# VectorE's two masked pieces ahead of ScalarE's four negated copies in each group of key products

## The chip, the cores and the metric

The kernel runs on one core of a Trainium2 chip. The metric is the device time of one execution in microseconds (us); times given for a kernel are medians over runs. TensorE multiplies matrices into PSUM, VectorE and ScalarE read PSUM and work element by element, GpSimd (POOL) works on SBUF alone, and SyncE (SP) issues transfers. In the rows PE is TensorE, PEld its weight loads, DVE VectorE and ACT ScalarE. Each engine works through its own list of instructions in order, and waits on semaphores for the others.

## The reference

A recurrent attention over 768 steps, whose state is a 40x40 matrix for each of 4 batches and 8 heads, and two gated layers behind it:

```python
for t in range(S):
    y[:, :, t] = np.einsum('bhd,bhde->bhe', rt, state)
    Sa = np.einsum('bhde,bhe->bhd', state, at)
    state_decay = state * wt[:, :, None, :] - np.einsum('bhd,bhe->bhde', Sa, bt)
    state = state_decay + np.einsum('bhd,bhe->bhde', vt, kt)
...
x = (silu(x @ w_gate) * (x @ w_val)) @ w_out        # 3072 x 320, d_ff 1536
x = (sigmoid(x @ w_gate) * (x @ w_val)) @ w_out
```

## The kernel before, in words

The 768 steps are cut into 12 chunks of 64. For a chunk, `prep_a` scales the keys by products of the decays, transposes them and forms **key products** (L486): four groups of four 128x128 products, each group in one PSUM tile `kps`. All chunks but the first use one PSUM bank (`mm`) for them, so the next group's products wait until the group before has been read out. Two things are read out of each group. ScalarE writes negated copies of blocks on the diagonal into `bn` (L495: 32 partitions by 4x64, L496: 32 by 4x32, for each of the two heads). VectorE writes masked pieces into `lq` (L498: 64 partitions by 4x64, one for each head).

`prep_b` inverts 1 + `bn` by blocks on VectorE: `halves` for chunks 0 to 2 (begins with the transpose L554, works in L567 and L573, ends with `x1t` at L578), `whole` for chunks 3 to 11 (begins with the transpose L512, works in 15 pairs of L526 and L532, ends with `x1t` at L536). TensorE makes `zps` and `xps` (L647) from it, and ScalarE writes the inverse X (L662). `chain` is the recurrence from chunk to chunk: products `qps` (L692, from the fourth chunk on L766), copies `qs` on ScalarE (L779), products `ups` with X (L710, later L787), copies of those (L800, L803), products `sps`, and the new state. `post` computes the chunk's outputs (aps L861, yps L892, `ysb` L906). Between them TensorE works off the first gated layer for the chunk before (`gv` L1112, `po` L1128), and VectorE, ScalarE and POOL turn float64 weights into pairs of fp32r tiles (on VectorE L1014, L1015, L1019, L1020, four passes for a third of a weight tile). When the 12 chunks are done the rest of the first layer and the second layer run as one stream of products (L1167, L1128).

Python generators are merged by fixed weights (`merge`), which gives each instruction a priority. A scheduler then lays the instructions out on the engines with those priorities and its own cost model, and places the semaphores. It lets two engines that read the same PSUM bank do so only one after the other, in the order in which they are written in the code. So the order of lines sets a chain of waits within a group, and moves what the scheduler puts around it.

Of the kernel before, what the change touches and what calls it, by code (L numbers as in the profile page):

```python
# [42 lines left out]
def attention(ctx, tc, st, ident, ins, banks, extra, early, more):  # L43
# [4 lines left out]
    nc = tc.nc  # L48
# [40 lines left out]
    QUAD = [slice(32 * j, 32 * j + 32) for j in range(4)]  # L89
# [128 lines left out]
    inv, done, out = {}, set(), {}  # L218
# [61 lines left out]
    for hs in HALF:  # L280
        nc.gpsimd.affine_select(
            out=mask[hs, :],
            in_=mask[hs, :],
# [20 lines left out]
    for u in range(2):  # L304
        nc.vector.tensor_reduce(
            out=odd[:, u : u + 1], in_=ident.rearrange("p (c u) -> p u c", u=2)[:, u], axis=AX.X, op=ALU.add
# [7 lines left out]
    for l in range(2):  # L314
        for z in range(2):
            nc.vector.tensor_reduce(
                out=sel[:, 2 * l + z : 2 * l + z + 1],
                in_=ident.rearrange("p (h l z c) -> p l z h c", h=2, l=2, z=2)[:, l, z],
# [131 lines left out]
    def prep_a(m):  # L450
        if 0 < m < FS:
            yield from scanned(m)
            if m == FS - 1:
                done.add("scans")
        elif m:
            while m not in rd:
                yield
            en = ends(m)
            s = scaled(m)
            next(s)  # L460
            next(en)
            yield
            yield from s
        tk = tkb[m % 3]
        while m > 2 and ("q", m - 3) not in done:
            yield
        for bp in range(2):
            ps = tr4(lambda n: an[:, 4 * bp + n])
            for h2 in range(2):
                e = E40[h2]  # L470
                nc.scalar.copy(
                    out=lq[m % 3][e, 8 * bp : 8 * bp + 8, h2], in_=ps[e].rearrange("p n (c t) -> p (n c) t", c=2)
                )
            yield
        if m >= FS:
            pends[m] = next(en)
        bn = wk.tile([P, NS, C], F32, tag="bn", name="bn", bufs=2)
        for g4 in range(4):
            q = slice(4 * g4, 4 * g4 + 4)
            ps = tr4(lambda n: tk[:, 4 * g4 + n], ("joined", None, "merged", None)[g4] if m == 1 else None)  # L480
            kbt = wk.tile([P, 4, P], F32, tag="kbt", name="kbt", bufs=1)
            nc.scalar.copy(out=kbt[0:PW], in_=ps[0:PW])
            pool, tag = ((pmm, "mm"), (pzy, "zy"), (pqu, "qu"), (po, "po1"))[g4 if m == 0 else 0]
            kps = pool.tile([P, 4, 2, C], F32, tag=tag, name="kps")
            for n in range(4):
                nc.tensor.matmul(  # L486
                    kps[:, n].rearrange("p h t -> p (h t)"),
                    lhsT=kbt[0:PW, n, :],
                    rhs=lq[m % 3][0:PW, 4 * g4 + n].rearrange("p h t -> p (h t)"),
                    start=True,  # L490
                    stop=True,
                )
            for h2 in range(2):
                lo, hi = QUAD[2 * h2], QUAD[2 * h2 + 1]
                nc.scalar.mul(out=bn[lo, q, :], in_=kps[lo, :, h2, :], mul=-1.0)  # L495
                nc.scalar.mul(out=bn[hi, q, 0:32], in_=kps[hi, :, h2, 32:64], mul=-1.0)  # L496
                o = HALF[1 - h2]
                nc.vector.tensor_tensor(  # L498
                    out=lq[m % 3][o, q, h2, :],
                    in0=kps[o, :, h2, :],  # L500
                    in1=mask[o, None, :].to_broadcast([64, 4, C]),
                    op=ALU.mult,
                )
            yield
        inv[m] = bn

# [447 lines left out]
    if NCH > 1:  # L954
        start.append((prep_a(1), *QA))
# [601 lines left out]
```

## Time and profile before

| | |
|---|---|
| time, median of 3 runs | 1272.05 us (1271.22 to 1274.35) |
| the profiled execution's own time | 1274.74 us |
| its span, first to last instruction | 1272.7 us |
| TensorE busy, matmul rows | 1185.2 us (93%) |
| VectorE busy | 687.8 us (54%) |
| ScalarE busy | 592.3 us (47%) |
| mean granted TensorE clock | 0.956 of full speed |

The profile is of one execution. Its rows are read in us from the span's start. In rows of waits "A <- B" means that A's engine stood idle until B had ended. A TensorE that is busy throughout a stretch bounds it; where it has idle time, the wait that ended last in front of it does.

### The profile page before, as it was taken

The page shows a single profiled execution, that of the slowest core. Times are in us where ns is not written, and L with a number is a line of the kernel's source. Part 1 is how long each engine was busy: PE and PEld are TensorE (multiplying, and loading weights), DVE is VectorE, ACT ScalarE, POOL GpSimd, SP SyncE. Part 2 cuts the span into 40 slices and gives each one's busy share as a digit, 9 for nine tenths or more (in the row PEclk, how much of TensorE's full clock was granted, in tenths as well). Part 3 has the DMA queues.
Part 4 walks back from the last instruction along what each step waited for, and adds up shares of the span by engine and source line. Part 5 has one row for each costly group of instructions (what it writes and reads, how often), then busy time and mean ns, then how long its engine had stood idle before and what let it go on. Part 6 is the DMA issues. An engine that isn't in the chain of part 4 may idle for free.

```text
span 1272.7 us, 31392 instructions
## 1 busy us (share of the span) xinstructions
PE 1185.2 (93%) x12545; PEld 1070.1 (84%) x12545; DVE 687.8 (54%) x1432; ACT 592.3 (47%) x1447; POOL 557.7 (44%) x749
## 2 busy tenths in 40 slices
PE   5598799999999999899999999999999999999997
PEld 4487588889889988788898888888888888888886
DVE  6867769876678667956867544467121212121111
ACT  8465546556655575455433433445232323232222
POOL 5744842233223224356855766676232223222221
PEclk8678868999999999999999999999999999999998
DMA  7444664544655555343464543323010101000001
GB/s 221 131 131 148 146 168 123 123 99 111 153 121 115 115 136 122 88 106 110 125 237 126 182 160 127 107 88 91 2 46 1 46 1 35 1 21 1 22 1 25
DMA packets 180460, 124.38 MB, mean 98 GB/s; under 512 B 134608, under 2 KB 160208, under 8 KB 179536
## 3 DMA queue, kind: packets, MB, share of 16 engines
q1 hardware_dynamic: 180144, 122.11, 35.5%
q8 instruction: 101, 1.65, 0.5%
q14 instruction: 55, 0.45, 0.1%
q10 hardware_dynamic: 160, 0.16, 0.1%
HBM read 90.81 MB, written 31.43 MB: 96 GB/s over the span
## 4 chain that ended last, share of the span: by engine, by line
PE 60%; DVE 22%; ACT 8%; issue 4%; DMA 2%; POOL 2%; SPq 0%; DVEq 0%; ACTq 0%; POOLq 0%
PE g L1167 31%; PE po L1128 16%; DVE pr L526 4%; PE gv L1112 4%; DVE part L532 3%; PE kps L486 2%; PE aps L861 2%; PE tp L371 2%; DVE lq L498 1%; PE ups L787 1%; ACT bn L496 1%; DVE am L870 1%; DVE dt L1015 1%; ACT bn L495 1%; ACT part L751 1%
## 5 line engine op out<-in xcount | busy, mean ns | idle before, releaser
L1167 PE MATMUL g<-x,w 128*128 128x512 f32 (+1 forms) x1792 | 419.8, 385 | 2.1 <-DVE g L1174 2.0
L1167 PEld LDWEIGHTS g<-x,w 128*128 128x128 f32 x1792 | 323.3, 188 | 62.8 <-issue 2.8
L1176 POOL TENSOR_TENSOR hl<-g,hh 128x256 fp32r<-128x256 f32 x216 | 162.1, 756 | 281.8 <-ACT hh L1175 253.9
L1174 DVE TENSOR_TENSOR g<-g,g 128x256 f32<-128x256 f32 x216 | 82.1, 419 | 342.4 <-PE g L1167 340.1
L1128 PE MATMUL po<-w,hh 128*128 128x320 f32 x1152 | 233.6, 311 | 0.9 <-ACT hh L1118 0.8
L1128 PEld LDWEIGHTS po<-w,hh 128*128 128x128 f32 x1152 | 187.0, 188 | 9.9 <-ACT hh L1118 1.0
L1175 ACT CAST hh<-g 128x256 fp32r<-128x256 f32 x216 | 86.9, 406 | 179.4 <-PE po L1128 169.7
L1112 PE MATMUL gv<-x,w 128*128 128x256 f32 x1152 | 165.6, 291 | 3.8 <-DVE g L1117 2.5
L1128 PE MATMUL po<-w,hl 128*128 128x320 f32 x576 | 151.1, 313 | 3.6 <-POOL hl L1119 3.5
L1112 PEld LDWEIGHTS gv<-x,w 128*128 128x128 f32 x1152 | 147.7, 192 | 6.8 <-DVE g L1117 3.9
L1171 ACT ACTIVATE g<-g 128x256 f32<-128x256 f32 x216 | 73.0, 382 | 149.5 <-PE g L1167 143.1
L1119 POOL TENSOR_TENSOR hl<-g,hh 128x256 fp32r<-128x256 f32 x72 | 62.8, 872 | 128.8 <-ACT hh L1118 127.9
L1032 POOL TENSOR_TENSOR dt<-dt,w 128x384 f32<-128x384 f32 (+1 forms) x72 | 80.3, 1116 | 87.5 <-ACT w L1030 42.7
L1128 PEld LDWEIGHTS po<-w,hl 128*128 128x128 f32 x576 | 99.6, 188 | 5.6 <-POOL hl L1119 5.2
L498 DVE TENSOR_TENSOR lq<-kps,part 64x256 f32<-64x256 f32 x96 | 40.5, 422 | 85.9 <-ACT bn L496 67.0
L526 DVE TENSOR_TENSOR pr<-part,sn 128x4 f32<-128x4 f32 (+4 forms) x135 | 76.2, 565 | 3.7
L1014 DVE TENSOR_SCALAR dt<-dt 128x384 int32<-128x384 int32 (+1 forms) x72 | 41.8, 580 | 52.8 <-POOL dt L1011 52.5
L486 PE MATMUL kps<-lq,kbt 104*128 104x128 f32 x384 | 61.3, 309 | 8.9 <-DVE lq L498 6.4
L532 DVE TENSOR_REDUCE part<-pr 128x2 f32<-128x4 f32 (+4 forms) x135 | 66.6, 493 | 2.8
L486 PEld LDWEIGHTS kps<-lq,kbt 104*128 104x128 f32 x384 | 53.4, 215 | 13.2 <-PE yps L892 4.1
L861 PE MATMUL aps<-rbd,ut 104*128 104x128 f32 x384 | 57.1, 295 | 6.1 <-DVE ysb L906 3.6
L1030 ACT CAST w<-dt 128x384 fp32r<-128x384 f32 (+1 forms) x72 | 35.6, 495 | 55.3 <-DVE dt L1015 48.2
(185 smaller groups left out, 1711.4 us busy)
## 6 DMA issues: line engine op xcount, KB each, us to landing
raw<-in_w_dram SPq DMA_DIRECT2D x48, 384.0 KB
xd<-x SPq DMA_DIRECT2D x12, 896.0 KB
x<-xd SPq DMA_DIRECT2D x11, 896.0 KB
raw<-in_w_dram SPq DMA_DIRECT2D x24, 320.0 KB
ld<-in_a_kb_dram SPq DMA_DIRECT2D x22, 320.0 KB
ld<-rd SPq DMA_DIRECT2D x64, 80.0 KB
pn<-pd SPq DMA_DIRECT2D x32, 160.0 KB
ld<-in_a_a_dram SPq DMA_DIRECT2D x12, 320.0 KB
```

What stands on the lines that cost most here:

```text
L486: nc.tensor.matmul(kps[:, n].rearrange("p h t -> p (h t)"), lhsT=kbt[0:PW, n, :], rhs=lq[m % 3][0:PW, 4 * g4 + n].rearrange("p h t -> p (h ...
L526: nc.vector.tensor_tensor(out=o, in0=xs[:, 0:kk, None, 0:n].to_broadcast([P, kk, 2, n]), in1=sn[:, None, n : n + 2, 0:n].to_broadcast([P, ...
L532: nc.vector.tensor_reduce(out=xs[:, 0:kk, n : n + 2], in_=o, axis=AX.X, op=ALU.add)
L861: nc.tensor.matmul(aps[:, n, h2], lhsT=ut[0:PW, x, 2 * h2 : 2 * h2 + 2].rearrange("p u s -> p (u s)"), rhs=rbd[0:PW, x, h2].rearrange("p b ...
L1032: sub(out=tf, in0=tf, in1=w.bitcast(F32), op=ALU.subtract)
L1112: nc.tensor.matmul(gv[n], lhsT=p, rhs=q, start=e == 0, stop=e == len(seq) - 1)
L1128: self.nc.tensor.matmul(ops[u], lhsT=p[:, us], rhs=q, start=first and n == 0, stop=last and n == 2)
L1167: nc.tensor.matmul(gv[k][:, 0:n], lhsT=p, rhs=cols(at), start=e == 0, stop=e == len(seq) - 1)
L1171: nc.scalar.activation(out=g[j], in_=gv[0][:, j], func=AF.Silu if silu else AF.Sigmoid)
L1174: nc.vector.tensor_tensor(out=g[j], in0=gv[1][:, j], in1=g[j], op=ALU.mult)
L1175: nc.scalar.copy(out=hh, in_=g[j])
L1176: self.heng.tensor_tensor(out=hl, in0=g[j], in1=hh.bitcast(F32), op=ALU.subtract)
```

## The change

In each group the loop over the two heads is split into two loops: first both masked pieces on VectorE, then the four negated copies on ScalarE. What each instruction reads and writes is the same.

```diff
             for h2 in range(2):
-                lo, hi = QUAD[2 * h2], QUAD[2 * h2 + 1]
-                nc.scalar.mul(out=bn[lo, q, :], in_=kps[lo, :, h2, :], mul=-1.0)
-                nc.scalar.mul(out=bn[hi, q, 0:32], in_=kps[hi, :, h2, 32:64], mul=-1.0)
                 o = HALF[1 - h2]
                 nc.vector.tensor_tensor(
                     out=lq[m % 3][o, q, h2, :],
...
                     op=ALU.mult,
                 )
+            for h2 in range(2):
+                lo, hi = QUAD[2 * h2], QUAD[2 * h2 + 1]
+                nc.scalar.mul(out=bn[lo, q, :], in_=kps[lo, :, h2, :], mul=-1.0)
+                nc.scalar.mul(out=bn[hi, q, 0:32], in_=kps[hi, :, h2, 32:64], mul=-1.0)
             yield
```

In the changed file the masked piece stands at L495, the copies at L503 and L504, and every later line is one higher. The instructions and their number are the same on every engine; their order differs from the first chunk until the last chunks.

VectorE in the opening of the program, before: the eight masked pieces of chunk 0 (`lq_192`), passes of the weight conversion (`dt`, `ds`) and scaled keys of chunk 1 (`part_88`, `tkb_90`), up to the transpose with which the inversion of chunk 0 begins (L554).

```order
L155 TENSOR_SCALAR s_1209<-s_1209 128x10x64
L498 TENSOR_TENSOR lq_192<-kps,part_86 64x4x64 x5
L418 TENSOR_TENSOR part_88<-ld,dtp 128x8x2x32
L498 TENSOR_TENSOR lq_192<-kps,part_86 64x4x64
L1014 TENSOR_SCALAR dt<-dt 128x384
L1015 SCALAR_TENSOR_TENSOR dt<-raw,dt 128x384
L498 TENSOR_TENSOR lq_192<-kps,part_86 64x4x64
L425 TENSOR_TENSOR tkb_90<-ld,dtp 128x8x2x16 x2
L1019 TENSOR_SCALAR ds<-dt 128x384
L498 TENSOR_TENSOR lq_192<-kps,part_86 64x4x64
L554 STREAM_TRANSPOSE sn<-bn 128x512
```

The same place of the changed kernel (the transpose is L555 there):

```order
L495 TENSOR_TENSOR lq_192<-kps,part_86 64x4x64 x2
L155 TENSOR_SCALAR s_1209<-s_1209 128x10x64
L495 TENSOR_TENSOR lq_192<-kps,part_86 64x4x64 x4
L418 TENSOR_TENSOR part_88<-ld,dtp 128x8x2x32
L495 TENSOR_TENSOR lq_192<-kps,part_86 64x4x64 x2
L425 TENSOR_TENSOR tkb_90<-ld,dtp 128x8x2x16 x2
L1015 TENSOR_SCALAR dt<-dt 128x384
L555 STREAM_TRANSPOSE sn<-bn 128x512
```

The masked pieces go in pairs, and two weight passes have moved behind the transpose.

VectorE at the end of an inversion in the middle of the program, before: the last steps of the inversion (L526, L532), between them the masked pieces of two groups of the chunk after (`lq_192`), outputs (`ysb`) and the last step's transpose.

```order
L532 TENSOR_REDUCE part_88<-pr 128x13x2
L498 TENSOR_TENSOR lq_192<-kps,part_86 64x4x64
L526 TENSOR_TENSOR pr<-part_88,sn 128x28x28
L498 TENSOR_TENSOR lq_192<-kps,part_86 64x4x64
L532 TENSOR_REDUCE part_88<-pr 128x14x2
L906 TENSOR_TENSOR ysb<-yps,pn 128x320
L906 TENSOR_TENSOR ysb<-yps,pn 128x64
L526 TENSOR_TENSOR pr<-part_88,sn 128x900
L498 TENSOR_TENSOR lq_192<-kps,part_86 64x4x64
L532 TENSOR_REDUCE part_88<-pr 128x15x2
```

The same inversion of the changed kernel (L527 and L533 are its steps, L907 the outputs):

```order
L533 TENSOR_REDUCE part_88<-pr 128x13x2
L871 TENSOR_TENSOR am<-aps,part_86 128x512
L527 TENSOR_TENSOR pr<-part_88,sn 128x28x28
L495 TENSOR_TENSOR lq_192<-kps,part_86 64x4x64 x2
L533 TENSOR_REDUCE part_88<-pr 128x14x2
L527 TENSOR_TENSOR pr<-part_88,sn 128x900
L907 TENSOR_TENSOR ysb<-yps,pn 128x320
L907 TENSOR_TENSOR ysb<-yps,pn 128x64
L533 TENSOR_REDUCE part_88<-pr 128x15x2
L495 TENSOR_TENSOR lq_192<-kps,part_86 64x4x64 x2
```

The first pair stands where the second piece stood, and the second pair behind the last step.

ScalarE at the same time, before, up to the copies `qs` from which the recurrence goes on (L779); `x` are casts for the gated layer.

```order
L495 ACTIVATE bn<-kps 32x256
L496 ACTIVATE bn<-kps 32x4x32
L1064 CAST x<-xtp 128x512
L1068 CAST x<-xtp 64x256
L1069 CAST x<-xtp 64x256
L495 ACTIVATE bn<-kps 32x256
L496 ACTIVATE bn<-kps 32x4x32
L779 COPY qs<-qps 128x320 x2
```

The same place of the changed kernel (`qs` is L780 there):

```order
L1065 CAST x<-xtp 128x512
L1069 CAST x<-xtp 64x256
L1070 CAST x<-xtp 64x256
L503 ACTIVATE bn<-kps 32x256
L504 ACTIVATE bn<-kps 32x4x32
L503 ACTIVATE bn<-kps 32x256
L504 ACTIVATE bn<-kps 32x4x32
L780 COPY qs<-qps 128x320 x2
```

All four copies of the second group now stand straight ahead of `qs`, and they come behind that group's pair on VectorE.

## Rows read from the trace of the kernel before

**Rows 1.** The page, chain that ended last, shares of the span by engine.

```profile
PE 60%; DVE 22%; ACT 8%; issue 4%; DMA 2%; POOL 2%; SPq 0%; DVEq 0%; ACTq 0%; POOLq 0%
```

**Rows 2.** Windows: stretch, length, busy us by engine, granted clock, DMA share, GB/s.

```profile
32.00:64.00 32.00, 16.11 (x478) 14.26 (x478) 27.47 (x57) 13.51 (x32) 24.11 (x31) 0.66 0.46 130
900.00:1000.00 100.00, 100.00 (x521) 87.59 (x520) 17.76 (x44) 31.61 (x86) 29.02 (x44) 1.00 0.06 15
```

**Rows 3.** Windows from the start, and of one period, ups to ups.

```profile
0.00:244.40 244.40, 193.79 (x3297) 172.89 (x3299) 185.91 (x380) 145.34 (x321) 126.99 (x173) 0.79 0.55 147
...
371.24:412.88 41.64, 40.20 (x671) 37.73 (x673) 31.01 (x64) 25.30 (x63) 12.29 (x15) 1.00 0.55 128
```

**Rows 4.** Waits of the whole span: us in total, times, longest.

```profile
DVE lq L498 <- ACT bn L496: 67.0, 45, 5.1
...
ACT bn L495 <- PE kps L486: 36.0, 26, 2.4
...
PE hps L588 <- DVE x1t L578: 9.1, 1, 9.1
...
PE kps L486 <- DVE lq L498: 6.4, 12, 1.1
```

**Rows 5.** VectorE's waits from 22 to 42 us.

```profile
DVE lq L498 <- ACT bn L496: 3.5, 4, 1.7
```

**Rows 6.** Instructions of tile kps: durations min/median/max in ns.

```profile
L495 ACT ACTIVATE bn<-kps x96: 357/375/379, 25.3 to 512.8; 32x256 f32<-32x256 f32 x96
L496 ACT ACTIVATE bn<-kps x96: 268/270/272, 25.6 to 513.1; 32x128 f32<-32x128 f32 x96
L498 DVE TENSOR_TENSOR lq<-kps,part x96: 406/420/429, 27.2 to 513.4; 64x256 f32<-64x256 f32 x96
```

**Rows 7.** Timeline of TensorE in one period: start, us, instructions, idle before.

```profile
373.18 1.16 PE L486 MATMUL kps<-lq,kbt 104*128 104x128 f32 x8
...
378.18 0.65 PE L371 MATMUL tp<-ident,tkb 128*104 128x128 f32 x4 [0.51 <-ACT part L755]
...
407.18 1.13 PE L486 MATMUL kps<-lq,kbt 104*128 104x128 f32 x8 [0.43 <-DVE lq L498]
...
412.81 0.89 PE L787 MATMUL ups<-qs,part 64*64 64x40 f32 x23
```

**Rows 8.** Timeline of ScalarE in the same period.

```profile
376.75 0.38 ACT L495 ACTIVATE bn<-kps 32x256 f32<-32x256 f32 x1 [0.49 <-DVE lq L498]
...
399.28 1.19 ACT L662 ACTIVATE part<-xps 32x512 f32<-32x512 f32 x2
...
411.09 0.75 ACT L779 COPY qs<-qps 128x320 f32<-128x320 f32 x2
```

**Rows 9.** Timeline of VectorE in the same period.

```profile
376.28 0.43 DVE L498 TENSOR_TENSOR lq<-kps,part 64x256 f32<-64x256 f32 x1 [4.65 <-ACT bn L496]
...
405.58 0.98 DVE L526 TENSOR_TENSOR pr<-part,sn 128x784 f32<-128x784 f32 x1
406.62 0.42 DVE L498 TENSOR_TENSOR lq<-kps,part 64x256 f32<-64x256 f32 x1
...
409.93 1.09 DVE L532 TENSOR_REDUCE part<-pr 128x30 f32<-128x900 f32 x1
```

**Rows 10.** Timeline of VectorE and TensorE in the opening.

```profile
35.42 0.56 DVE L1015 SCALAR_TENSOR_TENSOR dt<-raw,dt 128x384 int32<-128x384 int32 x1
...
37.14 0.35 DVE L1019 TENSOR_SCALAR ds<-dt 128x384 int32<-128x384 int32 x1
...
37.74 1.05 DVE L554 STREAM_TRANSPOSE sn<-bn 128x512 f32<-128x512 f32 x1
...
68.84 0.43 DVE L498 TENSOR_TENSOR lq<-kps,part 64x256 f32<-64x256 f32 x1
...
72.53 3.23 PE L710 MATMUL ups<-qs,part 64*64 64x40 f32 x56
...
87.80 1.06 DVE L554 STREAM_TRANSPOSE sn<-bn 128x512 f32<-128x512 f32 x1
```

## The prediction

> **What bounds the kernel now.** I read the chain that ended last first: TensorE holds 60% of it, VectorE 22%, ScalarE 8% [rows 1]. Then the windows, since that is a mean over stages. In the late stretch TensorE is busy for 100.00 of 100.00 us at full clock [rows 2]; nothing there waits, and the change touches nothing there. In the middle, one chunk of the recurrence after the other takes 41.64 us, of which TensorE works 40.20 [rows 3]; the period shown is one of six alike between 244.4 and 496.2 us. So 1.44 us a period are to be had there, at most some 9 in all. The first 244.40 us are another matter: TensorE works 193.79 of them [rows 3] and stands for 50.6, and between 32 and 64 us it is busy for half of the time at a clock of 0.66, while VectorE is busy for 27.47 of 32 [rows 2]. There VectorE's order decides.
>
> Last the waits. VectorE stood idle 67.0 us in front of masked pieces until a copy L496 had ended, and ScalarE 36.0 us in front of copies until products had ended [rows 4]. The first is not a loss of 67.0: most of it is time in which the group's products, too, were not there yet. What reaches TensorE is smaller: 6.4 us in 12 waits of products for a masked piece that frees the bank, and 9.1 us for the `x1t` of chunk 0 [rows 4].
>
> **What the change does, and what it costs.** No work is added: 96 pieces of 0.42 us, 96 copies of 0.375 and 96 of 0.27 [rows 6] before and after. A group is read out in 2 x 0.42 + 2 x 0.645 = 2.13 us either way, since the two engines take turns at the bank. The turns fall from three to one. A turn itself costs little: the piece that starts at 376.28 takes 0.43 [rows 9], and the copy behind it starts at 376.75 [rows 8], 0.04 us after its end; two turns fewer are some 0.08 us a group. What counts is what each engine does while it waits for its turn, and where the scheduler puts the group. Three places:
>
> Opening, chunk 0. The transposes of its inversion start at 37.74 [rows 10]. Two weight passes (0.56 and 0.35 us, rows at 35.42 and 37.14) go from in front of it to behind it: 0.9 us sooner [rows 10]. Of the 3.5 us that VectorE stood in front of masked pieces here [rows 5] the alternation goes, but the products of the third and fourth group still have to come; I take 0.8 of it (bounds 0 and 3.5). So the inversion starts some 1.7 us sooner, and `x1t`, for which TensorE waits 9.1 us [rows 4], about 2 sooner, as two of the passes that stood in front of it now follow.
>
> It is then given back. The products `ups` of chunk 0 start at 72.53 [rows 10], and need X. In the changed order the copies of X stand behind the second group's four negated copies, these behind the pair, and the pair behind four weight passes, which end at 68.8 today, where the first piece starts at 68.84 [rows 10]. 68.84 + 0.84 for the pair + 1.29 for the copies + 1.2 for X (the 1.19 of the later form [rows 8]) is 72.2. So `ups` start as now. Next, though, the fourth group of chunk 1 and its pair stand ahead of the sums of the state on VectorE, not behind them, and the inversion of chunk 1 that starts at 87.80 [rows 10] can start up to 4 us sooner. Outputs behind it move the other way in VectorE's order, and the products that need their bank with them. I carry half, 2.0 us; the bounds are 0 and 6 (4, and half as much again when chunk 2 repeats it).
>
> Middle, second group of a period. Its products wait for the bank until 407.18, 0.43 us idle [rows 7], because the second piece of the first group runs from 406.62 to 407.04 behind a step of the inversion that ended at 406.56 [rows 9]. In the changed kernel the pair stands behind that same step. Without the first piece in front of it the step ends some 0.45 sooner, at 406.1; then 0.84 for the pair and 1.29 for the four copies with their gaps: 408.3. The products start 1.2 us later than now. Should the inversion begin sooner, which it can by 0.35 as its last wait ahead is shorter, it is 0.9 later. Against that: at 376.75 ScalarE stands 0.49 us in front of a copy for its turn [rows 8], and 0.51 us of TensorE's idle time at 378.18 follow from it, through a copy that ScalarE makes right behind [rows 7]. The third group's products start at 373.18 [rows 7] and are there by 374.4, when VectorE is idle (4.65 us of idle time in front of the piece at 376.28 [rows 9]); the pair is done before ScalarE comes to the copies, so that the 0.5 goes. Net +0.4 to +0.7 us a period; I take 0.5. Three periods of the changed order have this form; one has the pair a step earlier (the bank is free at 407.3, not later than now), and gains 0.4; three have their products in another order, which I price at nothing (bounds -0.5 and +0.9, the best and the worst of the other forms). Together +1.1 us.
>
> Late stretch: 0, for TensorE's full windows cover it [rows 2].
>
> Sum: -2.0 + 1.1 = -0.9 us. On the profiled execution's 1274.74 us that is 1273.8; that execution lies 2.7 above the median of the runs, 1272.05. The forecast is made for the median: 1271.1 us. A difference below 0.3%, 3.8 us, can't be told from none.
>
> **The rivals.** *The opening carries on (faster).* The sooner start of chunk 1's inversion passes to chunk 2 and to the first regular period, because VectorE and ScalarE and not TensorE's work set the end there: 50.6 us of standing in [rows 3] speak for it. Against it: POOL's weight work and transfers have their own pace in the opening. Opening -6, middle 0: 1266 us.
>
> *The pair holds up the recurrence (slower).* In the changed order all four copies of the second group stand ahead of `qs`, and the pair they wait for stands behind the last step of the inversion, which runs from 409.93 to 411.02 [rows 9]. Pair 0.84, copies 1.29: 413.2, then 0.75 for `qs`, which now starts at 411.09 [rows 8]; less 0.35 for an inversion that begins sooner, and less 0.4 for the piece no longer on the way, it is 413.2. `ups` start at 412.81 now [rows 7]. So `qs` and the second group's wait both come out 0.4 to 0.9 later, and since the inversion's start hangs on the fourth group, which follows `ups`, the delay adds up by period. Seven periods at 0.9 are 6.3 us; with nothing gained in the opening, 1278.3 us. It decides from 0.55 us a period (3.8 by 7). Speaking against it: the 0.5 us that each period gets back between `ups` and the fourth group. The Trainium skill says the same of the mechanism (PSUM — Partial Sum Buffer, Engine vs sequencer instructions): ScalarE's and VectorE's queues are strict first-in first-out, so whatever stands behind a waiting copy waits too. The trace agrees: the copies behind the one at 376.75 ran late by its 0.49 us [rows 8].
>
> *It moves nothing that counts.* The scheduler has shifted hundreds of rows, but TensorE's work is the same and nearly fills the middle. This is my forecast's own case.
>
> **How the numbers follow.** Within 0.3% (1268.3 to 1275.8): 0.47; the carried gain and what lies beyond 0.3%: 0.28; the held-up recurrence: 0.25. The range reaches down to 1264.5, a little past the carried gain, and up to 1278, nearly the seven long periods; it leaves out the two cases together (0.2). The likeliest case's own range is 1268.3 to 1275.8.
>
> **What would show it.** Right: VectorE's wait for L496 is gone from the list of waits, and ScalarE waits for masked pieces instead; the first transposes start near 36.0 and the second near 84; the `ups` of the first chunk start at 72 to 73; the period is 41.3 to 42.2 us, with about 1 us of idle TensorE in front of the second group and none at the third group's transposes; the first regular `ups` start about 242 in place of 244.4. Wrong: a period over 42.2 us makes it slower, a start of the regular part before 239 makes it faster; a late stretch that is not the same length would mean that I looked in the wrong place.

## The result and the profile after

The changed kernel takes 1288.61 us (median of 4 runs, 1286.98 to 1292.85) against 1272.64 of the kernel before: a ratio of 1.0126, interval 1.011 to 1.0142. The forecast was 1271.1 in a range of 1264.5 to 1278. The profiled execution spans 1286.8 us, 14.1 more than before. In the changed kernel the masked pieces stand at L495, the copies at L503 and L504, and everything behind them has moved down by one line.

First the windows that answer to [rows 2, 3]: stretch, length, busy us by engine, granted clock, DMA share, GB/s.

```profile
0.00:254.60 254.60, 192.03 (x3308) 171.16 (x3308) 189.23 (x381) 145.20 (x322) 125.04 (x173) 0.81 0.52 142
32.00:64.00 32.00, 15.65 (x418) 13.86 (x414) 27.48 (x55) 12.64 (x31) 23.53 (x30) 0.66 0.46 124
254.60:295.80 41.20, 39.43 (x656) 37.22 (x656) 30.03 (x61) 22.99 (x56) 11.79 (x14) 0.96 0.56 128
295.80:341.00 45.20, 42.41 (x688) 39.55 (x687) 32.20 (x66) 27.31 (x69) 12.09 (x14) 1.00 0.54 123
341.00:385.70 44.70, 41.04 (x657) 38.79 (x656) 30.94 (x63) 24.63 (x62) 11.23 (x14) 0.92 0.54 115
385.70:428.00 42.30, 40.50 (x672) 37.81 (x671) 31.70 (x63) 24.90 (x63) 12.97 (x15) 1.00 0.46 109
...
470.22:513.44 43.22, 41.61 (x671) 39.20 (x670) 31.71 (x63) 25.35 (x64) 12.28 (x15) 0.96 0.50 114
513.44:562.29 48.85, 43.09 (x650) 39.91 (x650) 37.50 (x75) 23.24 (x57) 19.14 (x26) 0.86 0.37 101
900.00:1000.00 100.00, 100.00 (x523) 87.71 (x523) 19.85 (x48) 30.84 (x84) 31.23 (x45) 1.00 0.06 15
```

The first regular `ups` start at 254.60 in place of 244.3, 10.3 us late. The last ones start at 604.0 in place of 585.5, so that another 8.2 is lost between. From there to the end it is 682.8 us against 687.2 before: 4.4 come back. The late stretch is full, as it was. Period by period, from the first regular `ups` to the last (us):

| period | 1 | 2 | 3 | 4 | 5 | 6 | 7 | 8 |
|---|---|---|---|---|---|---|---|---|
| before | 43.55 | 41.66 | 41.63 | 41.64 | 41.65 | 41.64 | 46.37 | 43.00 |
| changed | 41.12 | 45.22 | 44.75 | 42.25 | 42.25 | 43.22 | 48.85 | 41.75 |

So plain periods are 42.25 long in place of 41.6. In the changed kernel the first has some 16 products of TensorE fewer in it, and the second as many more; the first, third and sixth have a granted clock below 1.00, and the seventh 0.86. The seventh of the kernel before, to be read against the 513.44 line above:

```profile
496.10:542.47 46.37, 39.65 (x650) 37.05 (x650) 37.08 (x76) 23.27 (x57) 18.71 (x26) 0.96 0.40 111
```

The waits that answer to [rows 4] (us in total, times, longest):

```profile
DVE lq L495 <- PE kps L486: 49.3, 24, 5.1
...
ACT bn L503 <- DVE lq L495: 19.1, 22, 2.1
...
PE kps L486 <- ACT bn L504: 13.4, 13, 3.6
...
PE hps L589 <- DVE x1t L579: 8.6, 1, 8.6
...
PE yps L893 <- DVE am L871: 3.3, 5, 0.8
```

VectorE's wait for a negated copy, 67.0 us before, is gone from the list, and its products are what VectorE waits for now. Where TensorE lost 6.4 us to masked pieces it now loses 13.4 to the copies behind them. And there is a wait that the forecast did not have: `yps` for `am`, the mask of `post`, 3.3 us in 5 times (1.0 in 2 before).

One plain period shows both. VectorE of the changed kernel (start, us, instructions, idle before), to be read against [rows 9]:

```profile
416.92 0.86 DVE L527 TENSOR_TENSOR pr<-part,sn 128x676 f32<-128x676 f32 x1
417.81 0.86 DVE L533 TENSOR_REDUCE part<-pr 128x26 f32<-128x676 f32 x1
418.59 0.68 DVE L871 TENSOR_TENSOR am<-aps,part 128x512 f32<-128x512 f32 x1
419.19 0.97 DVE L527 TENSOR_TENSOR pr<-part,sn 128x784 f32<-128x784 f32 x1
420.18 0.86 DVE L495 TENSOR_TENSOR lq<-kps,part 64x256 f32<-64x256 f32 x2
```

TensorE in the same stretch, against [rows 7]:

```profile
419.32 1.13 PE L893 MATMUL yps<-part,rbd 104*64 104x40 f32 x32 [0.77 <-DVE am L871]
...
422.45 1.16 PE L486 MATMUL kps<-lq,kbt 104*128 104x128 f32 x8 [0.81 <-ACT bn L504]
```

The second mask of `post` stands behind the reduction of 26 columns (in the kernel before it stands ahead of it), and TensorE waits 0.77 us for it. The pair stands behind the next step, the product of 784 columns; before the change only the second piece stood behind it [rows 9]. TensorE waits 0.81 us for the four copies that follow the pair, where it waited 0.43 [rows 7]. Of nine inversions with this step, the mask stands behind the reduction in none of the kernel before and in six of the changed one.

The opening, to be read against [rows 10]. VectorE, the two inversions' transposes:

```profile
36.29 1.08 DVE L555 STREAM_TRANSPOSE sn<-bn 128x512 f32<-128x512 f32 x1
...
89.44 1.06 DVE L555 STREAM_TRANSPOSE sn<-bn 128x512 f32<-128x512 f32 x1 [1.46 <-ACT bn L504]
```

TensorE, the first recurrence products of chunk 0:

```profile
73.50 1.80 PE L711 MATMUL ups<-qs,part 64*64 64x40 f32 x22 [0.29 <-ACT part L663]
```

The first inversion starts 1.45 us sooner, near the 1.7 of the forecast; in e17 below, with the same opening order, it starts at 37.87, so that a difference of this size is not clear of what executions differ by. `ups` start 1.0 later all the same, and the second inversion 1.6 later, where up to 4 sooner was forecast. The delay grows from there: the third inversion starts 4.2 later (130.51 for 126.34), the fourth 7.5 (178.91 for 171.45), and the first regular `ups` 10.3.

### The profile page after: what moved, and what is told of

Read it like the earlier page. It is cut to its first block, busy times and chain, and to the rows that moved or that the text cites. A ratio compares the mean times of both kernels' runs of the same rounds, so it can differ in the third digit from the quotient of the medians.

```text
span 1286.8 us, 31385 instructions
## 1 busy us (share of the span) xinstructions
PE 1190.5 (93%) x12545; PEld 1075.2 (84%) x12545; DVE 693.3 (54%) x1432; ACT 590.3 (46%) x1447; POOL 555.8 (43%) x749
## 4 chain that ended last, share of the span: by engine, by line
PE 63%; DVE 20%; ACT 7%; DMA 4%; issue 4%; POOL 2%; SPq 0%; ACTq 0%; DVEq 0%; POOLq 0%
PE g L1168 30%; PE po L1129 16%; PE gv L1113 5%; DVE pr L527 4%; DVE part L533 3%; PE kps L486 2%; PE aps L862 2%; PE tp L371 1%; PE qps L767 1%; PE ups L788 1%; DMA wt<-in_a_w_dram 1%; DVE am L871 1%; PE yps L893 1%; ACT bn L503 1%; DVE part L826 1%
## 5 line engine op out<-in xcount | busy, mean ns | idle before, releaser
L1177 POOL TENSOR_TENSOR hl<-g,hh 128x256 fp32r<-128x256 f32 x216 | 162.6, 758 | 282.4 <-ACT hh L1176 254.1
L527 DVE TENSOR_TENSOR pr<-part,sn 128x4 f32<-128x4 f32 (+4 forms) x135 | 78.0, 578 | 3.8
L486 PE MATMUL kps<-lq,kbt 104*128 104x128 f32 x384 | 62.5, 313 | 16.8 <-ACT bn L504 13.4
L533 DVE TENSOR_REDUCE part<-pr 128x2 f32<-128x4 f32 (+4 forms) x135 | 66.4, 492 | 2.7
L495 DVE TENSOR_TENSOR lq<-kps,part 64x256 f32<-64x256 f32 x96 | 40.5, 422 | 50.8 <-PE kps L486 49.3
L1009 ACT ACTIVATE dt<-raw 128x384 f32<-128x384 f32 (+1 forms) x72 | 38.3, 534 | 51.8 <-POOL w L1037 30.2
```

Of the source, the lines that this page charges most:

```text
L486: nc.tensor.matmul(kps[:, n].rearrange("p h t -> p (h t)"), lhsT=kbt[0:PW, n, :], rhs=lq[m % 3][0:PW, 4 * g4 + n].rearrange("p h t -> p (h ...
L527: nc.vector.tensor_tensor(out=o, in0=xs[:, 0:kk, None, 0:n].to_broadcast([P, kk, 2, n]), in1=sn[:, None, n : n + 2, 0:n].to_broadcast([P, ...
L533: nc.vector.tensor_reduce(out=xs[:, 0:kk, n : n + 2], in_=o, axis=AX.X, op=ALU.add)
L1177: self.heng.tensor_tensor(out=hl, in0=g[j], in1=hh.bitcast(F32), op=ALU.subtract)
```

## The experiments

Seventeen kernels, all compared with the kernel before on the same chip. In most, a group's copies and piece of head `h2` are made two small functions, and one line chooses their order by chunk `m` or group `g4` (here for e1):

```diff
-            for h2 in range(2):
+            for step, h2 in (((piece, 0), (piece, 1), (copies, 0), (copies, 1)) if m < 5 else ((copies, 0), (piece, 0), (copies, 1), (piece, 1))):
+                step(h2)
```

What came out; the ratio is to the kernel before in the same set of runs, "first" and "last" are the starts of the first and the last regular `ups` in us, "plain" is the length of the plain periods in the profile, the short ones that are nearly alike, in brackets those of others between the first period and the last two. The last three columns are of one profiled execution, which for e7 is 5.7 us and for e9 4.5 us slower than the median beside it, for the others at most 2.5 off it.

| run | pieces first where, or edit | median us | ratio, interval | first | plain | last |
|---|---|---|---|---|---|---|
| before | | 1272.64 | 1 | 244.3 | 41.6 | 585.5 |
| changed | always | 1288.61 | 1.0126, 1.0110 to 1.0142 | 254.6 | 42.3 (45.2, 44.7, 43.2) | 604.0 |
| e1_early | `m < 5` | 1277.84 | 1.0046, 1.0032 to 1.0061 | 254.4 | 41.7 | 591.8 |
| e2_late | `m >= 5` | 1282.97 | 1.0079, 1.0048 to 1.0110 | 244.4 | 42.2 (44.6) | 597.1 |
| e3_chunks01 | `m in (0, 1)` | 1291.83 | 1.0152, 1.0119 to 1.0185 | 253.6 | 41.6 | 600.6 |
| e4_chunks12 | `m in (1, 2)` | 1275.52 | 1.0024, 1.0005 to 1.0043 | 247.5 | 41.6 | 588.6 |
| e5_first_group | `m >= 5 and g4 == 0` | 1276.18 | 1.0028, 1.0013 to 1.0043 | 244.1 | 41.5 | 585.7 |
| e6_second_group | `m >= 5 and g4 == 1` | 1279.16 | 1.0057, 1.0033 to 1.0081 | 239.4 | 41.3 (42.4, 45.3) | 585.0 |
| e7_copies_pair | `m >= 5`, copies first | 1282.57 | 1.0073, 1.0048 to 1.0099 | 243.4 | 42.0 (45.0, 42.6) | 597.1 |
| e8_not_first_group | `m >= 5 and g4` | 1282.93 | 1.0078, 1.0055 to 1.0102 | 242.7 | 41.4 (43.4, 44.5) | 591.7 |
| e9_mask_ahead | `m >= 5`, mask placed | 1279.80 | 1.0062, 1.0040 to 1.0084 | 245.2 | 41.1 (42.6, 44.9) | 590.8 |
| e10_pass_behind | always, one pass placed | 1302.26 | 1.0236, 1.0209 to 1.0263 | 257.7 | 42.2 (44.7) | 611.3 |
| e11_chunk0 | `m == 0` | 1285.45 | 1.0113, 1.0085 to 1.0142 | 254.1 | 41.7 | 596.3 |
| e12_heads_swapped | never; second head first | 1274.29 | 1.0017, 0.9997 to 1.0036 | 244.2 | 41.8 | 588.5 |
| e13_chunk0_solve_first | `m == 0`, solve placed | 1280.46 | 1.0067, 1.0045 to 1.0089 | 251.4 | 41.6 | 593.5 |
| e14_all_solve_first | always, solve placed | 1315.15 | 1.0326, 1.0298 to 1.0354 | 261.4 | 43.5 to 45.3 | 619.0 |
| e15_before_solve_first | never, solve placed | 1277.92 | 1.0046, 1.0028 to 1.0065 | 247.4 | 41.7 | 592.4 |
| e16_mask_and_pool | `m >= 5`, mask and POOL placed | 1274.95 | 1.0017, 1.0000 to 1.0034 | 244.8 | 41.1 | 582.3 |
| e17_all_middle_mended | always, mask and POOL placed | 1275.10 | 1.0020, 1.0003 to 1.0037 | 253.5 | 41.1 | 588.8 |

**Which part of the program loses.** e1 to e4 were one set.

> Pieces ahead of copies in chunks 0 to 4 alone, whose key products all lie before the regular part (40 of the 96 pieces); chunks 5 to 11 keep the old order. Opening theory: the loss is made before the first regular products, +10.3 us there in the changed kernel (244.3 to 254.6), so this kernel loses 8 to 14 us, 1281 to 1287, and its periods are 41.6 long again. Pair theory (each group's pair holds up what stands behind it, evenly): 40/96 of 16.0 = 6.7 us, 1279.

> The other part alone: pieces ahead of copies in chunks 5 to 11 (56 of 96 pieces), the opening as before. Opening theory: first regular products at 244 as before, and then only the 0.6 us that a plain period is longer in the changed kernel (42.2 for 41.6), seven times: 4 us, 1274 to 1278. Pair theory: 56/96 of 16.0 = 9.3 us, 1282, with the long periods (44.7, 45.3, 48.8) here too.

The opening theory missed both. e1 has all of the opening's delay at the first regular `ups` and yet loses 6.0 us, not 8 to 14; e2 has the opening of before, and loses 11.1, not 4. The pair theory's shares come near (6.7 and 9.3); e3 to e6 do not bear out its even spread. The loss of e2 lies in the periods, of which some are 42.2 long and others 44.6. One of each:

```profile
288.60:330.80 42.20, 40.41 (x670) 37.75 (x669) 31.69 (x63) 24.99 (x63) 12.54 (x15) 1.00 0.53 122
375.50:420.00 44.50, 42.88 (x672) 40.45 (x671) 31.68 (x63) 24.99 (x63) 12.51 (x15) 0.92 0.48 108
```

The same instructions with the same pauses, but in the second TensorE is busy 2.5 us longer, at a clock of 0.92. So it is in the period ahead of it; the third long one, from 420.0, has the clock at 1.00, 13 products more and three pauses of 0.7 to 1.0. The second in steps of 2 us (length, TensorE's busy time, granted clock, DMA share, GB/s):

```profile
407.50:409.50 2.00, 1.23 (x23) 1.00 0.15 43
409.50:411.50 2.00, 1.86 (x57) 1.00 0.67 203
411.50:413.50 2.00, 1.34 (x6) 0.58 0.55 125
413.50:415.50 2.00, 2.00 (x21) 0.50 0.45 80
415.50:417.50 2.00, 2.00 (x43) 0.50 1.19 202
417.50:419.50 2.00, 2.00 (x28) 0.71 0.43 63
```

Two pauses of 0.77 and 0.80 us, the wait for the mask and that for the copies, stand 3 us apart, and the clock is then at its lower level, 1.2 in place of 2.4 GHz, for some 6 us. In the period from 288.60 the same two pauses stand at the same distance, and the clock stays up. So a pause of this length costs 0.8 us or, in some periods, 0.8 and 2.3 more. The forecast had a pause in front of the second group's products, not the one for the mask, and not the second price.

> Pieces ahead of copies in chunks 0 and 1 alone (16 of 96 pieces). In the order of ScalarE that this gives, the weight pass that waited 4.2 us for its transfer in the changed kernel stands ahead of the second half's copies of the first recurrence products, as there. Theory of the misplaced pass: most of the opening's loss returns with it, 6 to 12 us, 1279 to 1285. Pair theory: 16/96 of 16.0 = 2.7 us, 1275.

> Pieces ahead of copies in chunks 1 and 2 alone (16 of 96 pieces). In the order of ScalarE that this gives, the same weight pass stands behind both halves' copies of the first recurrence products, as in the kernel before. Theory of the misplaced pass: no wait for its transfer in front of those copies, and nearly none of the opening's loss, -2 to +3 us, 1271 to 1276. Pair theory: 2.7 us as for chunks 0 and 1, 1275; the two theories part at the difference between the two kernels, 6 us or more against none.

They part by 16 us, in the direction of the misplaced pass; but chunks 0 and 1 alone lose 20.0 us, by the medians more than all chunks together (16.0; the two intervals overlap), which no theory of mine had. Which of the two differences between the kernels (chunk 0 or the pass) makes it was left to e10 and e11.

**The middle: pairs, or where they fall.** e5 to e8.

> Pieces ahead of copies in the first group of each of chunks 5 to 11 alone (7 groups); all else as before. The run with chunks 5 to 11 showed plain periods of 42.2 us and others of 44.5, in which TensorE stood 0.8 us for a mask of post (am) and 0.8 us for the copies that free the bank of this group, and then ran at a granted clock of 0.50 for some 6 us. Theory A (the first group's pair, queued on VectorE behind an inversion step, makes the pauses, the pauses bring the clock down): here VectorE's order keeps the mask ahead of the step, so one pause of 0.8 in place of 0.4 is left, a period of 41.6 to 42.2, and at most some dips; 1272 to 1277. Theory B (any writing by pairs costs, 11 us for 28 groups): a quarter, 2.8 us, 1275, spread over all periods with the clock at 1.00.

> Pieces ahead of copies in the second group of each of chunks 5 to 11 alone. Theory A: the first group's products and the masks of post keep their places, so no pause grows and the clock stays at 1.00: periods of 41.6, 1270 to 1273; a period longer only if the copies of the negated state keys now stand ahead of the copy of qs, by 0.4 to 0.8 us each as my forecast's rival had it (1275 to 1278). Theory B: 2.8 us, 1275.

In e5 the plain periods are 41.5 and in e6 41.3 us long, at a clock of 1.00: a pair by itself is no slower than two turns. Theory A holds in its main point, B (2.8 us spread over all periods) falls by the periods. By the times alone they don't part: 1276.2 of e5 fits both, and 1279.2 of e6 lies above both. That e5 and e6 lose 3.3 and 6.3 us nevertheless does not come from the plain periods: in e5 the last `ups` start as before and the loss stands behind them, and in e6 two periods are long by a cause that e9 shows.

> The opposite pairing in chunks 5 to 11: ScalarE's four copies first, then VectorE's two pieces. VectorE's order keeps both masks of post where they were, and TensorE's second group waits for the pair of pieces and not for copies. If the loss comes from writing by pairs at all (one engine ends its four before the other begins), it is as large as with pieces first: 44 us periods, about 1283. If it comes from the mask of post and the pair standing behind the inversion step (Theory A), one pause of 0.8 or so is left and the clock stays up: periods of 41.6 to 42.2, 1272 to 1277.

> Pieces ahead of copies in the second, third and fourth groups of chunks 5 to 11 (21 groups), the first group as before. In the order on VectorE that this gives, the second mask of post again stands behind the inversion step of 26 columns, as in the run with chunks 5 to 11, but the first group's pieces move too, behind the last steps. Theory A: pauses in front of the second group's products stay or grow, and the clock falls in some periods: 42 to 45 us a period, 1276 to 1284. Theory B: 21/28 of 11 us, 1280, at a clock of 1.00.

e7 gave the time of one rival (1282.6) with the plain periods of the other (42.0; one of 45.0 at a clock of 0.92), and did not decide. e8 lost as much as either theory had it, with the clock down in some periods as A said; but three plain periods of it are 41.3 to 41.5 long, and the loss sits in the three ahead of them (47.4, 43.4, 44.5) and, by 4.5 us, behind the last `ups`. In those short periods, too, the second mask stands behind the reduction of 26 columns, and TensorE does not wait for it, as other products stand ahead of `yps` there. So it is the wait that costs, and not the place by itself.

e9 is e2 with one instruction placed: the reduction of 26 columns behind the second mask of `post`, by a bound on VectorE's order without a semaphore.

```diff
-            nc.vector.tensor_reduce(out=xs[:, 0:kk, n : n + 2], in_=o, axis=AX.X, op=ALU.add)
+            red = nc.vector.tensor_reduce(out=xs[:, 0:kk, n : n + 2], in_=o, axis=AX.X, op=ALU.add)
+            if kk == 13:
+                behind(red, f"am{m - 2}")
...
+                if bp == 1 and g2 == 1 and m >= 2: marks[f"am{m}"] = msk
```

> Chunks 5 to 11 by pairs, as in the run of those chunks, with one order more on VectorE: the reduction of 26 columns of each inversion is placed behind the second mask of post, where it stands in the kernel before. The pair of the first group then stands one inversion step earlier too. Theory A (mask and pair behind an inversion step make the pauses; the clock follows from them): no wait of 0.8 for the mask, the clock at 1.00 in the plain periods, 41.3 to 41.8 us each, and the 11 us of the run with chunks 5 to 11 nearly gone: 1270 to 1276. Theory B (writing by pairs costs by itself): still 42 to 45 us a period, 1280 to 1284.

The waits for the mask are gone, and three periods are 41.1, half a microsecond shorter than before the change. The pair moves one step ahead with the mask, as was expected, and the wait for the copies is 0.64 in place of 0.80; the run does not part the two. And two of five such periods are long (42.6 and 44.9). The first 1.4 to 1.5 us of that is two instructions, the state updates. VectorE of e9 in the period of 42.6:

```profile
339.51 2.39 DVE L833 TENSOR_TENSOR part<-part,pend 104x320 f32<-104x320 f32 x2
```

POOL of e9 at the same time:

```profile
339.04 1.57 POOL L391 TENSOR_TENSOR part<-ld,pn 128x640 f32<-128x640 f32 x1 [7.94 <-DMA ld<-rd]
340.57 0.97 POOL L1127 TENSOR_TENSOR hl<-g,hh 128x256 fp32r<-128x256 f32 x1
```

In the kernel before, POOL in such a period:

```profile
334.26 1.55 POOL L391 TENSOR_TENSOR part<-ld,pn 128x640 f32<-128x640 f32 x1 [4.57 <-DMA xd<-part]
```

And VectorE's state updates there:

```profile
338.59 0.90 DVE L826 TENSOR_TENSOR part<-part,pend 104x320 f32<-104x320 f32 x2
```

The two state updates take 0.90 us with POOL idle beside them, and 2.39 when POOL's product runs at the same time: they end at 341.90, just behind POOL's two, which end at 341.54. The updates start 8.9 us behind the period's first `ups` in e9 and 9.1 in the kernel before; POOL's product starts 8.4 behind them in e9, released by another transfer (`ld`), and 4.7 in the kernel before. So the two have come to coincide. In the changed kernel itself they do not in the first six periods (each update 0.45 to 0.5 us): this came up when the mask was placed, and is no part of the loss there. The Trainium skill (SBUF — State Buffer, Who interferes with whom) says that VectorE and GpSimd share one pair of ports, as an exclusive lock; the trace agrees, with 2.39 for 0.90.

e16 adds a bound for POOL's product, behind the state update of the same period, with a semaphore:

```diff
-        nc.gpsimd.tensor_tensor(out=pairs(an), in0=heads(xa), in1=heads(pn), op=ALU.mult)
+        first = nc.gpsimd.tensor_tensor(out=pairs(an), in0=heads(xa), in1=heads(pn), op=ALU.mult)
+        if f"state{m - 3}" in marks:
+            tied([first], [marks[f"state{m - 3}"]])
...
+                marks[f"state{m}"] = nc.vector.tensor_tensor(
```

> Chunks 5 to 11 by pairs, the second mask of post ahead of the inversion step (as in the run before of that name), and POOL's product of the decayed inputs (128x640, 1.57 us) of chunk m bound behind the state update of chunk m-3. Theory P (the long state updates come from POOL working beside them, and the clock falls behind some of them): state updates of 0.9 us for the two in all periods, no period of 42.6 or 44.9, five or six of about 41.1; last recurrence products 3 to 6 us sooner than in that run, 1273 to 1277. Rival (the pairs make every second period long by themselves): the two long periods stay, 1278 to 1282.

Theory P holds. POOL of e16, in the period that answers to the one above:

```profile
336.51 1.56 POOL L391 TENSOR_TENSOR part<-ld,pn 128x640 f32<-128x640 f32 x1 [1.90 <-DVE part L835]
```

VectorE's state updates there:

```profile
335.54 0.89 DVE L835 TENSOR_TENSOR part<-part,pend 104x320 f32<-104x320 f32 x2
```

Windows of e16, that period, and from the last regular `ups` on:

```profile
326.70:367.80 41.10, 39.96 (x671) 37.73 (x671) 31.55 (x64) 25.24 (x63) 11.96 (x15) 1.00 0.54 123
...
582.30:592.30 10.00, 6.51 (x89) 6.00 (x90) 6.20 (x11) 5.27 (x14) 7.53 (x10) 0.85 0.26 77
582.30:1275.30 693.00, 676.45 (x3931) 601.07 (x3931) 255.24 (x550) 247.08 (x645) 309.59 (x432) 0.99 0.22 68
```

All five plain periods are 41.1 at full clock, and the last regular `ups` start at 582.3, 3.2 us sooner than before. Yet the time is no better than before (1.0017, interval 1.0000 to 1.0034): from the last `ups` on it takes 693.0 us against 687.2, and the first 10 of them have TensorE at work for 6.51 (all 10 in the kernel before). What is won in the periods is given back where the recurrence ends. What sets the pace there was not tried.

**The opening.** e10 to e15.

> Pieces ahead of copies in chunk 0 alone (8 of 96 pieces): the step of my forecast that was to start the first inversion 1.7 us sooner. In ScalarE's order here the weight pass stands behind the first recurrence products' copies. If the forecast's opening term is right where the pass does not interfere: inversion near 36.0, second inversion no later than 87.8, 1268 to 1273. If a sooner first inversion brings a loss by itself (weight passes and transfers moved behind it are missed later): first regular products at 247 or later, 1276 to 1284.

Chunk 0 alone, 8 of 96 pieces, delays the regular part by 9.8 us and the end by 13.8, more than chunks 0 to 4 together in e1 (6.0), though the weight pass stands behind the copies there. The opening term of the forecast has the wrong sign even where the pass does not stand in the way.

e10 is the changed kernel with the eighth weight pass bound behind the second half's last copy:

```diff
+            if m == 0 and hb == 1:
+                marks["w0"] = last
...
+            if len(count) > 7:
+                behind(x, "w0")
```

> All chunks by pairs, the changed kernel, with the weight pass that waited 4.2 us for its transfer placed behind the second half's copies of the first recurrence products on ScalarE. Theory of the misplaced pass: the 4.2 us in front of those copies go and the second half's products of chunk 0 end near 79 in place of 83.8; what follows keeps that gain, first regular products at 248 to 251 in place of 254.6, 1281 to 1285. Rival (the opening is late for its whole new order and its low clock): the pass moves and the regular part still starts at 253 or later, 1287 to 1291.

Moving the pass makes the changed kernel some 14 us slower, not faster. It does start the second inversion sooner (86.57 for 89.44, of which 1.9 are there at the first inversion already), but the third 11.4 later (141.93 for 130.51): the scheduler's answer behind the pass outweighs it. So e10 does not price the 4.17 us for which ScalarE waited there; that the pass is not needed for the delay is what e11 shows.

What e11 shows around the solve of chunk 0, ScalarE:

```profile
65.70 0.59 ACT L482 COPY kbt<-tp 104x512 f32<-104x512 f32 x1
66.31 0.37 ACT L495 ACTIVATE bn<-kps 32x256 f32<-32x256 f32 x1
66.69 0.27 ACT L496 ACTIVATE bn<-kps 32x128 f32<-32x128 f32 x1
66.99 1.16 ACT L669 COPY zt<-zps 32x512 f32<-32x512 f32 x2
```

In the kernel before, `zt` is copied at 64.55, ahead of the copies of chunk 1's first group. In e11 these and the next `kbt` stand ahead of it, and X is 2.2 us later. The second inversion is not late in e11 (87.75), the third is by 9.0 (135.32). e13 to e15 place the first products of chunk 1 behind `zps` of chunk 0, and its second transposes behind `xps`, and give chunk 1's key products a later priority (`QA`):

```diff
-            ps = tr4(lambda n: tk[:, 4 * g4 + n], ("joined", None, "merged", None)[g4] if m == 1 else None)
+            ps = tr4(lambda n: tk[:, 4 * g4 + n], ("joined", "merged1", "merged", None)[g4] if m == 1 else None)
...
+                if m == 1 and g4 == 0 and n == 0:
+                    behind(x, "zps")
...
-    QA = (0.3328, -0.4)
+    QA = (0.3328, 0.8)
```

> Chunk 0 alone by pairs, and two places in TensorE's order put back as in the kernel before: the first key products of chunk 1 behind zps of chunk 0, and the transposes for its second key products behind xps. Theory S (chunk 1's key products ahead of chunk 0's solve make the loss): zt is copied at 64 to 65 in place of 66.99, the first ups start at 70 to 72.5, the regular part at 242 to 248, 1269 to 1277. Rival (the sooner start itself, through weight passes and the clock): regular part at 252 or later, 1282 to 1288.

> All chunks by pairs, with the same two places put back. Theory S: regular part at 244 to 249 in place of 254.6; the middle keeps its own loss of 8 to 11 us (as in the run with chunks 5 to 11), so 1279 to 1285. Rival: regular part at 252 or later, 1287 to 1293.

> The kernel before with the same two places bound, which there changes the order only behind them (the second transposes wait for xps, which they mostly did). If binding costs nothing by itself: 1269 to 1276, regular part at 243 to 247. If it costs several us here, the two runs above have to be read against this one and not against the kernel before.

In e13 the first `ups` start at 70.9, sooner than in any kernel until then, but the second inversion only at 94.40, and the regular part at 251.4: 2.7 us of the 9.8 come back. e15 shows that these edits cost 6.5 us by themselves, and e14, where all of it came together, took 1315 us, with the regular part at 261.4. Read against e15, as its expectation asked, chunk 0 by pairs costs 2.5 us and delays the regular part by 4.1 (e13), and all chunks by pairs cost 37 and 14.1 (e14). So theory S is neither shown nor excluded: the edits move more than what they were meant to move.

> Neither order changed: copies and piece stay head by head, but the second head of each group goes first, in all chunks. The durations are the same and the number of turns too, so each theory of the turns gives no change: 1270 to 1275. It shows how far an exchange that costs nothing moves the rest of the order: if the time goes up by 4 us or more, the scheduler's answer to any exchange here is worth more than what the exchange itself does.

As expected, and its interval holds 1. This exchange, which keeps the turns, moves little.

**How the two parts add up.** e17 is the changed kernel, its opening untouched row by row, with the two places of e16.

> The changed kernel, all chunks by pairs, its opening untouched row by row, with the second mask of post ahead of the inversion step and POOL's product behind the state update from chunk 5 on. If the opening's loss and the middle's are separate: regular part from 254 to 255 as in the changed kernel, plain periods of 41.1 at a clock of 1.00, last recurrence products near 594 in place of 604.0; and as the run before gave back in the last two periods and behind them what the middle had gained, 1278 to 1286. If the two hang together (the opening's phase makes the middle's collisions in another place): periods over 42 remain, 1286 or more.

```profile
0.00:253.50 253.50, 191.22 (x3294) 170.39 (x3294) 188.21 (x381) 144.07 (x320) 124.36 (x173) 0.80 0.51 141
335.80:376.90 41.10, 39.94 (x671) 37.70 (x671) 31.57 (x64) 25.07 (x63) 11.98 (x15) 1.00 0.54 122
...
588.80:1273.40 684.60, 671.03 (x3931) 596.76 (x3930) 256.30 (x551) 248.50 (x646) 313.11 (x434) 1.00 0.22 69
```

It came out better than expected: 1275.1, 3.5 us above the kernel before in its set. So 12.5 of the 16.0 us are gone with two places in the middle, though the regular part starts 9.2 us late. With the opening of before the same two places take e2's 11.1 us down to e16's 1.5. Read the other way, the opening's pairs cost 2.0 us with the middle mended (e17 against e16), 4.9 with it unmended, and 6.0 alone (e1). The two places were not tried in the kernel before by itself; its mask stands ahead already, and its state updates take 0.90 in each period of 41.6. In this profile the delay is made up by a first period of 41.2 (43.6 before), five plain ones of 41.1 (41.6), one of 43.8 behind them (46.4), and 2.6 us less from the last `ups` on; only the last period is longer, 44.9 for 43.0.

## Why the prediction was wrong, step by step

- *No work is added, a turn costs 0.04 us*: right. The pair's two pieces take 0.86 together, and plain periods with pairs are 41.1 long where mask and pair stand ahead of the product of 784 columns (e9, e16, e17).
- *Opening, inversion of chunk 0 1.7 us sooner, `x1t` 2 sooner*: 1.45 and 0.7 (52.72 for 53.40), both within what executions of one order differ by (e17). The wait for `x1t` fell from 9.1 [rows 4] to 8.6.
- *`ups` at 72 to 73, as now*: 73.50. The reason given, that they stand behind the second group's copies, is what the trace shows.
- *Second inversion up to 4 us sooner, 2.0 carried*: wrong in sign. It starts at 89.44, and the first regular `ups` 10.3 later. I carried a sooner start along a chain and did not follow what the scheduler put into the room, such as chunk 1's key products ahead of chunk 0's own solve; how much of the delay that is stays open (e11 to e15). In place of -2.0 the opening alone costs 6.0 (e1). But this is the smaller loss: with a delay as large, e17 is 3.5 us above the kernel before in its set of runs.
- *The period before, 41.64, one of six alike*: there are five of them; the first of the six is 43.6 long.
- *Middle: second group's products 0.9 to 1.2 later, net +0.4 to +0.7 a period*: right in size for the two plain periods in which the clock holds (42.25 for 41.6), and in part by luck. The wait in front of the second group grew by 0.4 only (0.81 for 0.43), the third group's 0.51 went as forecast, with another of 0.30, and the 0.77 for the mask, which I had not seen, came in.
- *Middle, +1.1 in all*: **this is the step that failed.** The chunks of the middle alone cost 11.1 (e2); in the changed kernel they lost 8.2 up to the last `ups`, and with the middle mended 12.5 us of the result were gone. Of the terms of that sum, the three periods of the known form came out at +0.6, +0.6 and +1.6 where +0.5 each stood (periods 4 to 6); the one with the pair a step earlier at +3.1 where -0.4 stood (period 3); of the three in another order, priced at nothing, two (periods 1 and 2) at -2.4 and +3.6, so +1.1 together, and the third lies ahead of the first regular `ups`. The seventh period, which the sum did not have, lost 2.5, and the last was 1.3 shorter. Three things were missing. The second mask of `post` falls behind the reduction of 26 columns in six of nine inversions, which the order of instructions showed and I did not look for, since I followed the pieces and copies and not what they displaced. Behind two pauses of 0.8 near each other the clock fell to 0.50 in some periods, 2.3 us more in e2, and in the sixth period here some 1.0 (0.96 for 1.00); I priced waits at full clock. That the pauses bring the clock down is read from rows and was not tested by itself. And in period 3, from 341.0 to 385.7, the copies stood behind a copy of `ob` that waited 3.69 us for a transfer, and TensorE waited 3.59 for them. ScalarE there:

```profile
376.39 0.43 ACT L1384 COPY ob<-po 128x320 f32<-128x320 f32 x1 [3.69 <-DMA xs<-ob]
376.72 0.37 ACT L503 ACTIVATE bn<-kps 32x256 f32<-32x256 f32 x1
```

And TensorE:

```profile
378.09 2.07 PE L486 MATMUL kps<-lq,kbt 104*128 104x128 f32 x8 [3.59 <-ACT bn L504]
```

- *Late stretch 0*: right for the full windows; the remainder behind the last `ups` is 4.4 shorter, which the forecast named as a sign of having looked in the wrong place.
- *The rival that the pair holds up the recurrence, 1278.3*: its side was right and its size too small. In the changed kernel TensorE's regular `ups` wait for `qs` 0.8 us in 2 times, against 1.6 in 2 before; in e16 they wait 2.4 in 5, and the periods are shorter all the same. So that mechanism did not decide. The faster rival, a gain carried through the opening, has the wrong side.

Open remain: which part of the opening's delay is order and which the lower clock (64 to 96 us: 0.74 before, 0.50 in the changed kernel; neither was changed alone), why e3 with nearly the same first regular `ups` as e1 ends 14 us later (in the profiles 7.3 of it is the first period, 48.0 for 40.8, and 4.6 lies behind the last `ups`), and what limits the stretch behind the last `ups`.

## What to carry to other kernels

Where a scheduler lays out the order, look in the new order for what the moved instructions displaced, above all for short ones that TensorE then waits for, before pricing what the change itself does. Price a pause of TensorE twice, with the clock held and with the clock fallen. When a stretch gets shorter, ask which instruction of another engine with its own pace (a product that follows a transfer) it now runs into.

## What the runs showed that was not expected

- The clock: two pauses of 0.77 and 0.80 us were followed by 0.50 for some 6 us in one period and by 1.00 in another of the same execution. In e14 seven of eight regular periods had a mean clock of 0.96 or less.
- The same order of the opening can run 5 us sooner: in e6 each engine's order is nearly that of the kernel before as far as 235 us, and the first regular `ups` started at 239.4 in place of 244.3, with a clock of 0.87 between 160 and 192 us, where the profile of before shows 0.61.
- A VectorE instruction of 128x256 with two SBUF inputs (0.48 us elsewhere) took 5.33 us at the third inversion of the changed kernel, beside POOL's products without a break, and as long in e1, e3 and e17, which share that stretch of the order. In the kernel before it took 0.55 there, also beside such products, and in e11, as late at the regular part, 1.47: so it is not what that delay needs, and why it differs stays open.
